# Moving operand, weight-sum and weight-split work inside a gated-MLP / channel-MLP kernel on one core

## The chip, the cores and the metric

The kernel runs on one core of one Trainium2 chip. A core has four compute engines that the profile names PE (matrix products), DVE, ACT and POOL (GpSimd), a queue SP that issues nearly all transfers of this kernel, and 16 DMA engines that carry them. The metric is the time of one execution on the device, in microseconds (us); lower is better.

## The reference, cut to what matters

```python
def reference(...):
    attn_out = favor attention of q, k, v            # 8 batches, 8 heads, 576 tokens
    x = attn_out as [8, 576, 512]
    # gated MLP
    h = relu(x @ w_in); u, v = halves of h
    v_n = normalised v over its features
    gated = u * (w_spatial @ v_n + b_spatial)
    x = gated @ w_out
    # token mixing of rank 32, then channel MLP
    u = x + (x^T @ U @ V)^T
    ch = relu(u @ w_ch1) @ w_ch2                      # 512 -> 2048 -> 512
    return u + ch
```

The inputs `w_ch1` and `w_ch2` come in a 64-bit form that the kernel must first turn into float32; it calls that fetching or repacking a weight.

## The kernel before, in words

The kernel runs in three parts, one behind the other: attention (to about 420 us), the gated MLP, batch by batch for 8 batches of some 63 us, and the channel MLP. The last batch of the gated MLP overlaps with the start of the channel MLP.

Every product is made in split precision. `split` makes a high part of an operand (a cast, on ACT at line 145 or on DVE at line 147) and a low part (source minus high part, line 148, on DVE in all places that matter here), and `products` multiplies three combinations of them.

The channel MLP uses seven block products where a 2 x 2 block product has eight (`PRODUCTS`). Left operands are sums of weight blocks, formed on POOL by `left_sums` (line 437, four operations a block) and then split into tiles `cw` (first matrix, also called w1) or written to memory as `w2d` and loaded again as `w` (second matrix). Right operands are sums of activation blocks: `right_parts` loads a batch as `u`, forms the differences `t` on POOL (`less`, line 1075) and splits the seven operands into tiles `us` (ACT, then DVE). What comes out of the inner products (`ph_x`, `ph_y`, `ph_z`) is added up on DVE as `c` (line 1138), goes through the ReLU on ACT as `h`, and becomes the right operand of the outer products, whose differences `t` (POOL) and splits `hc` (ACT, DVE) are made by `operands`. The outer products fill `pc`; DVE adds them to `r` (line 1300).

The hidden width of 2048 is taken in two halves of 1024. Each half and each of the 8 batches makes one outer pass, so there are 16, numbered from 0. A pass has 28 outer groups of six matmuls (`OUTER`: seven products, four tiles `t` each), and behind nearly every outer group one inner group of six matmuls of the pass to come. The program order in the channel MLP is written out by hand and kept (`put`): the order of the code is the order on each engine.

The weights are prepared in three places:

- In gated batches 1 to 6 `work()` is called eight times a batch (four times in the gate's first loop, twice in its second, twice around the mixing products), and each call does the next step of a job and, where that ends it, begins another. A job is the turning of a piece of `w_ch1` or `w_ch2` into float32 (`fetch_weight`: `raw_c` loaded, `low_c` and `bits_c` computed), or, for batches 1 to 4, `pair(m)`, which forms the first half's sums of w2 and stores them (`w2s` to `w2d`).
- The first half's w1 sums are made in the last gated batch, in the transition to the channel MLP: `fetch_pair(m)` loads the raw blocks `ca`, `combine(m)` forms the sums `cs` on POOL and splits both into `cw`, for m = 0 to 3.
- The second half's sums of both matrices are made by `second_group`, 41 steps of 8 weight blocks (one step of sums on POOL, four steps of splits `cd` on ACT and DVE whose results are stored). `channel` takes one step behind each of the seven outer products of a pass, from the middle of pass 0 on, until they are used up in pass 6.

`channel` first runs the inner products `7 * GROUP + LEAD - 7 * EARLY` steps ahead (six groups beyond the first batch's), then starts pass 0. In the last batch of the gated MLP `gated_out` makes each token tile's products `px`, copies them to `x` on ACT (line 940; the last product of a tile is line 770), splits `x` into `xh` and `xl` on DVE, and `low_rank` multiplies these into `pr`.

Of the kernel before, what the change touches and what calls it, by code (L numbers as in the profile page):

```python
# [9 lines left out]
F32 = mybir.dt.float32  # L10
# [8 lines left out]
P = 128  # L19
# [5 lines left out]
LEAD = 6  # L25

# [73 lines left out]
class Mixer:  # L100
# [3 lines left out]
    def __init__(self, tc, ctx, aps):  # L104
# [31 lines left out]
        self.w1x = dp.tile([P, GROUP, 2, 7, 2 * P], F32, name="w1x")  # L136
# [207 lines left out]
    def channel_jobs(self):  # L344
# [78 lines left out]
        jobs = jobs[3 * GROUP :]  # L423
        n = len(todo) - GROUP
        for i in range(n):
            todo[GROUP + i] = jobs[i::n]
# [438 lines left out]
    def gate(self, b, jobs):  # L865
# [27 lines left out]
        for f in range(self.KH):  # L893
# [20 lines left out]
            if f < self.KH - 2:  # L914
                self.work()
# [74 lines left out]
    def alloc_channel(self, es):  # L990
        tc = self.tc
        pool = lambda name: es.enter_context(
            tc.tile_pool(name=name, bufs=1, side="right")
        )
        cw, self.hu, hp, self.cst = [pool(n) for n in ("cw", "hu", "hp", "cst")]
        self.cw, self.hp = [cw] * 3, [hp]
        self.w1, self.h, self.us, self.raw = {}, {}, {}, {}

    def alloc_outer(self, es):
# [3 lines left out]
        self.cw.append(pool("cv"))  # L1003
        self.hp.append(pool("hq"))
        self.w2p, self.hc, self.ot = [pool(n) for n in ("w2p", "hc", "ot")]
        self.ps["c"] = pool("psc", space=PSUM, reuse_waits="tile")

    def fetch_raw(self, kind, m):

        a = self.cst.tile([P, 4, 2 * P], F32, tag="c32a", name=f"ca{kind}_{m}", bufs=1)  # L1010
# [12 lines left out]
    def fetch_pair(self, m):  # L1023
        self.raw[m] = self.fetch_raw(1, m)
# [5 lines left out]

    def combine(self, m):

        a = self.raw.pop(m)
        z = self.sums_of(a, m)
        w = self.first_left(m)
        flat = w.rearrange("p i x k c -> p i x (k c)")
        self.split(flat[:, 0, :3], flat[:, 1, :3], a[:, :3], elo="dve")
        self.split(flat[:, 0, 3:], flat[:, 1, 3:], z, elo="dve")

    def first_left(self, m):  # L1040
        t = m % GROUP
        w = self.cw[t].tile([P, 2, 7, 2, P], F32R, tag=f"w{t}", name=f"cw{m}", bufs=1)
        self.w1[m] = w
        return w

    def second_group(self):
# [5 lines left out]
        for n, (kind, m) in enumerate(blocks):  # L1052
# [3 lines left out]
            for x, k, src in ((0, 2, a[:, :2]), (2, 1, a[:, 2:3]), (3, 2, z[:, :2]), (5, 2, z[:, 2:])):  # L1056
                d = self.w2p.tile([P, 2, 2, 2 * P], F32R, tag="cd", name=f"cd{kind}_{m}_{x}", bufs=2)
                self.split(d[:, 0, :k], d[:, 1, :k], src, elo="dve")
                for i in range(2):
                    dst = (  # L1060
                        self.w1x[:, t, i, x : x + k, :] if kind == 1
# [16 lines left out]
    def right_parts(self, n, u):  # L1078
# [452 lines left out]
```

## Time and profile before

| | before |
|---|---|
| median of 3 runs | 1668.12 us (1666.5 to 1670.28) |
| the profiled execution's own time | 1674.35 us |
| its span in the trace | 1672.6 us |
| PE busy | 1589.4 us, 95% of the span |
| DVE busy | 1146.1 us, 69% |
| ACT busy | 877.5 us, 52% |
| POOL busy | 792.8 us, 47% |
| mean granted clock of PE over the span | 0.981 |

The span is what the profile shows from the first to the last instruction. The profiled execution took 1.75 us more than its span and 6.2 us more than the median of the timed runs. A busy PE is not always PE at full speed: where the granted clock is below 1.00, matmuls run longer, so both PE's idle time and its clock have to be read. A mean clock below 1.00 is a mixture of two levels, 2.4 and 1.2 GHz.

### The profile page before, as it was taken

Reading aid. Unit: us, or ns where it says so; the run is one execution under the profiler, and the core shown is the slowest. Engines: PE = TensorE matmul, PEld = TensorE weight load, DVE = VectorE, ACT = ScalarE, POOL = GpSimd, SP = SyncE. Lnnn points to the kernel's source line nnn. Section 1 sums busy time; section 2 is a strip of 40 time slices with the busy share of each in tenths; the row PEclk is TensorE's granted clock in tenths of the full one; section 3 lists DMA queues with packets and bytes.
Section 4 is the critical chain, followed back from the end, with each engine's and each line's share of the span. In section 5 each row is a group of like instructions: output and inputs, shape, how many; then the busy total and the mean of one; then the engine's idle time right before and its main releaser. Section 6 shows DMA issues by size and latency. Waiting matters only on the chain.

```text
span 1672.6 us, 30522 instructions
## 1 busy us (share of the span) xinstructions
PE 1589.4 (95%) x11592; PEld 1484.4 (89%) x11592; DVE 1146.1 (69%) x1642; ACT 877.5 (52%) x1668; POOL 792.8 (47%) x610
## 2 busy tenths in 40 slices
PE   7999999999999999999997989999989999999998
PEld 7998988988889789788786889999989999999998
DVE  5888757855567767757637567777766776666665
ACT  4888767873344344344334455555544455444453
POOL 2678766774334334334234436654543444443442
PEclk9999999999999999999997999999999999999999
DMA  4677766642143343343213669889989867777776
GB/s 131 178 208 206 205 185 185 195 139 86 56 154 106 106 154 103 109 123 91 84 58 116 198 215 302 294 289 310 305 285 374 263 219 230 233 250 241 244 239 231
DMA packets 169302, 322.04 MB, mean 193 GB/s; under 512 B 25474, under 2 KB 96290, under 8 KB 166596
## 3 DMA queue, kind: packets, MB, share of 16 engines
q1 hardware_dynamic: 169012, 320.03, 60.4%
q8 instruction: 91, 1.49, 0.4%
q14 instruction: 55, 0.45, 0.1%
q10 hardware_dynamic: 144, 0.07, 0.0%
HBM read 244.24 MB, written 66.21 MB: 186 GB/s over the span
## 4 chain that ended last, share of the span: by engine, by line
PE 61%; DVE 12%; DMA 10%; ACT 7%; issue 5%; POOL 4%; SPq 1%; DVEq 0%; POOLq 0%; ACTq 0%
PE pc L758 16%; PE ph_x L758 9%; PE pn L595 4%; PE ph_z L758 4%; PE pv L758 4%; PE pkv L567 4%; PE pu L758 3%; DMA raw_c<-in_w_ch 3%; POOL t L1075 2%; PE ph_y L758 2%; PE px L758 2%; DVE us L148 2%; PE pk L494 2%; DMA w<-w2d 2%; PE pt L526 1%
## 5 line engine op out<-in xcount | busy, mean ns | idle before, releaser
L758 PE MATMUL pc<-hc,w 128*128 128x288 f32 x2688 | 427.1, 298 | 9.7 <-DVE hc L148 3.7
L758 PEld LDWEIGHTS pc<-hc,w 128*128 128x128 f32 x2688 | 383.8, 190 | 12.4 <-ACT hc L145 4.8
L758 PE MATMUL ph_x<-us,cw 128*128 128x288 f32 x1536 | 252.0, 301 | 12.6 <-ACT u L1133 10.6
L548 POOL TENSOR_TENSOR qp<-e,qp 128x576 fp32r<-128x576 f32 x128 | 183.5, 1455 | 120.6 <-ACT e L545 94.8
L758 PEld LDWEIGHTS ph_x<-us,cw 128*128 128x128 f32 x1536 | 222.2, 192 | 16.9 <-ACT u L1133 13.6
L1075 POOL TENSOR_TENSOR t<-h,h 128x576 f32<-128x576 f32 x64 | 95.7, 1496 | 254.0 <-DVE hc L148 223.9
L595 PE MATMUL pn<-qp,kv 128*65 128x288 f32 x768 | 207.7, 331 | 7.7 <-DVE nd L604 4.0
L148 DVE TENSOR_TENSOR hc<-t,hc 128x576 fp32r<-128x576 f32 x128 | 127.0, 994 | 76.9 <-ACT hc L145 76.2
L567 PE MATMUL pkv<-v,kp 128*128 128x65 f32 x1024 | 155.2, 255 | 0.0
L567 PEld LDWEIGHTS pkv<-v,kp 128*128 128x128 f32 x1024 | 153.9, 194 | 0.0
L1146 ACT ACTIVATE h<-c 128x288 f32<-128x288 f32 x192 | 85.6, 446 | 127.9 <-DVE c L1138 127.8
L1133 ACT COPY u<-ph_x 128x288 f32<-128x288 f32 x128 | 51.0, 398 | 171.5 <-PE ph_x L758 171.1
L758 PE MATMUL ph_z<-us,cw 128*128 128x288 f32 x768 | 126.7, 301 | 11.9 <-DVE c L1138 11.9
L758 PEld LDWEIGHTS ph_z<-us,cw 128*128 128x128 f32 x768 | 110.4, 191 | 15.4 <-DVE c L1138 15.1
L148 DVE TENSOR_TENSOR hc<-h,hc 128x576 fp32r<-128x576 f32 x96 | 116.6, 1230 | 3.4 <-ACT hc L145 3.1
L1075 POOL TENSOR_TENSOR t<-h,t 128x576 f32<-128x576 f32 x64 | 112.0, 1751 | 8.3 <-DVE hc L148 5.8
L1075 POOL TENSOR_TENSOR t<-u,t 128x576 f32<-128x576 f32 x32 | 56.7, 1773 | 124.5 <-DVE us L148 123.2
L758 PE MATMUL pz<-wt,vn 128*128 128x288 f32 x768 | 112.7, 296 | 0.2
L595 PEld LDWEIGHTS pn<-qp,kv 128*65 128x65 f32 x768 | 99.6, 140 | 13.5 <-ACT nd L606 5.6
L758 PE MATMUL pu<-xs,wi 128*128 128x288 f32 x768 | 104.8, 298 | 3.6 <-DVE v L822 3.6
L758 PEld LDWEIGHTS pu<-xs,wi 128*128 128x128 f32 x768 | 104.1, 190 | 4.6 <-DVE v L822 3.9
L1300 DVE TENSOR_TENSOR r<-pc,r 128x576 f32<-128x576 f32 x112 | 84.5, 755 | 33.2 <-PE pc L758 31.9
(169 smaller groups left out, 3166.4 us busy)
## 6 DMA issues: line engine op xcount, KB each, us to landing
w<-w2d SPq DMA_DIRECT2D x224, 512.0 KB, 4.6
u<-ud SPq DMA_DIRECT2D x16, 1152.0 KB, 5.8
raw_c<-in_w_ch SPq DMA_DIRECT2D x32, 512.0 KB, 4.1
v<-in_v SPq DMA_DIRECT2D x32, 325.0 KB, 4.1
k<-in_kT SPq DMA_DIRECT2D x32, 320.0 KB, 3.4
q<-in_qT SPq DMA_DIRECT2D x32, 320.0 KB, 4.1
x<-nd SPq DMA_DIRECT2D x64, 144.0 KB, 3.4
rec<-rd SPq DMA_DIRECT2D x64, 144.0 KB, 3.2
```

What stands on the lines that cost most here:

```text
L148: return self.put((nc.gpsimd if elo == "pool" else nc.vector).tensor_tensor(out=lo, in0=src, in1=hi, op=ALU.subtract))
L494: self.pin(nc.tensor.matmul(pa[:, j * NF + t, :], x[d, t * P : (t + 1) * P], ws[d, :], start=True, stop=True,))
L526: self.pin(nc.tensor.transpose(pt[:, at, :], s[:, u, :], self.ident))
L548: self.pin(nc.gpsimd.tensor_tensor(out=lo[:, c], in0=e[:, c], in1=hi[:, c], op=ALU.subtract))
L567: self.pin(nc.tensor.matmul(pkv[:, i, j, :], kp[:, j * NF + t, :], vb[:, u * D1 : (u + 1) * D1], start=False, stop=(j == 1 and t == NF - 1),))
L595: self.pin(nc.tensor.matmul(pn, kv[k][:, i, g // 2, :], qp[q][:, i, g * HS : (g + 1) * HS], start=(m == 0), stop=(m == len(terms) - 1),))
L758: self.put(self.nc.tensor.matmul(out, x, y, start=(start and i == 0), stop=(stop and i == len(terms) - 1), skip_group_check=chained,))
L1075: self.put(self.nc.gpsimd.tensor_tensor(out=out, in0=p, in1=q, op=ALU.subtract))
L1133: self.put(nc.scalar.copy(out, src))
L1146: self.put(nc.scalar.activation(self.h[n, t // 2, x][:, t % 2], src, AF.Relu))
L1300: self.put(nc.vector.tensor_tensor(out=r, in0=pc, in1=r, op=ALU.add))
```

## The change

Five things are changed.

1. The first half's w1 sums move from the transition into gated batch 6. A new job `left(m)` loads the raw blocks, forms the sums, splits them in two parts (tiles `w1s`) and stores them in `w1x[0]`; the last batch then only loads the four finished tiles with `load_left`. `fetch_pair`, `combine` and `first_left` are gone. Batches 1 to 4 now repack four pieces and do a `pair` (before three and a `pair`), batch 5 repacks the last eight, and batch 6 does the four `left` jobs (before, batches 5 and 6 repacked six pieces each in turn). `work()` is called once more in a batch, in the gate's second loop.
2. `right_parts` forms the next batch's operands in another order (product 2 before product 1; `t3` before the split of product 1 and `t6` behind it), and begins at inner product (2, 2) instead of (3, 0), so its steps are spread over 16 inner products instead of 11.
3. The 41 weight steps of the second half are taken at outer groups 0, 2, 4, ..., 12 of the 28 of a pass, from pass 1 on, instead of at every fourth group of the whole pass from the middle of pass 0 on. They still end in pass 6.
4. Pass 0 begins four inner groups sooner (`FIRST = 2` instead of 6 ahead); the four are made up behind its groups 3, 7, 11 and 15. In the first products (2, 0) moves behind (1, 5) and (1, 6).
5. Pools: `cw`'s four tags stand in one pool, `h` in pools by pair and by parity, and `cst` is taken with the outer pools. The numbers of buffers are in effect the same.

The core of the diff:

```diff
@@ channel_jobs
-        todo = [[] for _ in range(self.B - 2)]
-        for m in range(GROUP):
-            todo[m] = jobs[3 * m : 3 * m + 3] + [pair(m)]
...
+        def left(m):
+            def load():
+                w = self.mq.tile([P, 4, self.DM // 2], F32, tag="w2", name=f"w1_{m}", bufs=1)
+                self.raw_blocks(w, 1, m)
+                return lambda: sums(w)
+            def sums(w):
+                z = self.mq.tile([P, 4, self.DM // 2], F32, tag="z2", name=f"z1_{m}", bufs=1)
+                self.left_sums([w[:, x] for x in range(4)], z)
+                return part(w, z, 0)
+            def part(w, z, k):
+                n, src = (4, z) if k else (3, w[:, :3])
+                d = self.mq.tile([P, 2, 4, self.DM // 2], F32R, tag="w2s", name=f"w1s_{m}_{k}", bufs=1)
+                self.split(d[:, 0, :n], d[:, 1, :n], src, elo="dve")
+                for i in range(2):
+                    nc.sync.dma_start(
+                        self.w1x[0][:, m, i, 3 * k : 3 * k + n], d[:, i, :n].bitcast(F32)
+                    )
+                return (lambda: part(w, z, 1)) if k == 0 else None
+            return load
+        todo = [jobs[4 * m : 4 * m + 4] + [pair(m)] for m in range(GROUP)]
+        todo += [jobs[4 * GROUP :], [left(m) for m in range(GROUP)]]
@@ gate
-            if f < self.KH - 2:
+            if f < self.KH - 1:
                 self.work()
@@ new
+    def load_left(self, m):
+        g, t = divmod(m, GROUP)
+        w = self.cw.tile([P, 2, 7, 2, P], F32R, tag=f"w{t}", name=f"cw{m}", bufs=1)
+        self.nc.sync.dma_start(
+            w.bitcast(F32).rearrange("p i x k c -> p i x (k c)"), self.w1x[g][:, t]
+        )
+        self.w1[m] = w
@@ right_parts
+        part(2, t1)
+        yield
+        t3 = self.less(new(3), b22, b12)
+        yield
         part(1, t2)
         yield
-        part(2, t1)
         t6 = self.less(t2, b21, t2)
-        yield
-        t3 = self.less(new(3), b22, b12)
@@ inner
-        spread = {(3, 0), (2, 5), (3, 2), (3, 3), (3, 4), (4, 0), (3, 5), (3, 6), (4, 1)}
+        begin = {(2, 3): 1, (2, 5): 1, (2, 6): 1, (3, 6): 2, (4, 0): 2, (4, 2): 1, (4, 3): 1, (4, 4): 1}
+        spread = {
+            x: 1 for x in (
+                (2, 2), (2, 4), (2, 5), (3, 2), (3, 3), (3, 4), (4, 0), (3, 5), (4, 1), (4, 3),
+            )
+        }
@@ channel
-        for _ in range(7 * GROUP + LEAD - 7 * EARLY):
+        for _ in range(7 * GROUP + FIRST - 7 * EARLY):
             next(inner, None)
...
-                    for _ in range((0, 1, 0, 3)[t] if x == 3 else 1):
+                    pulls = (0, 1, 0, 3)[t] if x == 3 else 1
+                    at = GROUP * OUTER.index(x) + t
+                    if n == 0 and at in (3, 7, 11, 15):
+                        pulls += (LEAD - FIRST) // 4
+                    for _ in range(pulls):
                         next(inner, None)
-                if n or OUTER.index(x) > 2:
-                    next(later, None)
+                    if n and at in range(0, 14, 2):
+                        next(later, None)
@@ last gated batch
-            mx.fetch_pair(0)
-            right_parts = mx.right_parts(0, mx.load_chunk(0))
+            u = mx.load_chunk(0)
+            for m in range(GROUP):
+                mx.load_left(m)
+            right_parts = mx.right_parts(0, u)
```

Below, the orders of instructions on an engine show what the change moves. A name such as `hc_5_0` is a tile of outer product 5; the long number behind a name is a counter.

DVE in pass 2, before, behind the outer products whose sums are `r_11`; `us_4` are splits of the next batch's operands, `cd` a weight step's split, and `c_3` the sum that frees the bank for which a later inner product `ph_z` waits:

```order
L1300 TENSOR_TENSOR r_11_11550<-pc_0_11483,r_11_11550 128x576
L1300 TENSOR_TENSOR r_11_11550<-pc_2_11728,r_11_11550 128x576
L148 TENSOR_TENSOR us_4_11869<-u_4_11541,us_4_11869 128x576
L148 TENSOR_TENSOR us_4_11879<-t_4_11767,us_4_11879 128x576
L148 TENSOR_TENSOR us_4_11890<-t_4_11765,us_4_11890 128x576
L148 TENSOR_TENSOR cd_6_5_11894<-cs_6_11561,cd_6_5_11894 128x512
L148 TENSOR_TENSOR hc_5_0_11899<-h_2_0_10907,hc_5_0_11899 128x576
L1138 TENSOR_TENSOR c_3_11919<-ph_3_z,u_3_11888 128x288
L148 TENSOR_TENSOR us_4_11937<-t_4_11921,us_4_11937 128x576
L148 TENSOR_TENSOR hc_5_1_11940<-h_2_2_11187,hc_5_1_11940 128x576
L1138 TENSOR_TENSOR c_3_11957<-ph_3_z,u_3_11866 128x288
```

The same place after:

```order
L1320 TENSOR_TENSOR r_11_11569<-pc_0_11487,r_11_11569 128x576
L1320 TENSOR_TENSOR r_11_11569<-pc_2_11751,r_11_11569 128x576
L149 TENSOR_TENSOR us_4_11896<-t_4_11728,us_4_11896 128x576
L149 TENSOR_TENSOR us_4_11916<-t_4_11730,us_4_11916 128x576
L149 TENSOR_TENSOR hc_5_0_11919<-h_2_0_10911,hc_5_0_11919 128x576
L1153 TENSOR_TENSOR c_3_11939<-ph_3_z,u_3_11914 128x288
L149 TENSOR_TENSOR us_4_11956<-t_4_11906,us_4_11956 128x576
L149 TENSOR_TENSOR hc_5_1_11959<-h_2_2_11219,hc_5_1_11959 128x576
L1153 TENSOR_TENSOR c_3_11976<-ph_3_z,u_3_11893 128x288
```

Ahead of `hc_5_0` and `c_3` stand now two splits `us_4` where three splits and a `cd` stood; the first of the three (from `u_4`) and the `cd` are taken earlier in the pass. In the passes without weight steps the same place reads the same without the `cd` lines.

DVE at the beginning of the last gated batch's mixing, before; `cw` and `ca`, `cs` belong to `combine`, `xh` and `xl` to the token tiles that `low_rank` waits for, `us_0` to the first batch's operands:

```order
L148 TENSOR_TENSOR cw_9707<-ca_0_9656,cw_9707 128x768
L148 TENSOR_TENSOR cw_9707<-cs_9702,cw_9707 128x1024
L147 CAST xh_0_9694<-x_0_9693 128x512
L147 CAST xh_1_9722<-x_1_9721 128x512
L148 TENSOR_TENSOR xl_0_9695<-x_0_9693,xh_0_9694 128x512
L148 TENSOR_TENSOR xl_1_9723<-x_1_9721,xh_1_9722 128x512
L148 TENSOR_TENSOR us_0_9730<-u_0_9661,us_0_9730 128x576
L147 CAST xh_2_9734<-x_2_9733 128x512
L148 TENSOR_TENSOR us_0_9742<-u_0_9661,us_0_9742 128x576
L148 TENSOR_TENSOR xl_2_9735<-x_2_9733,xh_2_9734 128x512
```

The same place after:

```order
L148 CAST xh_0_9775<-x_0_9774 128x512
L149 TENSOR_TENSOR xl_0_9776<-x_0_9774,xh_0_9775 128x512
L148 CAST xh_1_9788<-x_1_9787 128x512
L148 CAST xh_2_9800<-x_2_9799 128x512
L149 TENSOR_TENSOR xl_1_9789<-x_1_9787,xh_1_9788 128x512
L149 TENSOR_TENSOR xl_2_9801<-x_2_9799,xh_2_9800 128x512
L149 TENSOR_TENSOR us_0_9796<-u_0_9734,us_0_9796 128x576
L149 TENSOR_TENSOR us_0_9808<-u_0_9734,us_0_9808 128x576
L148 CAST xh_3_9812<-x_3_9811 128x512
L149 TENSOR_TENSOR us_0_9830<-t_0_9783,us_0_9830 128x576
```

The splits of `cw` are gone and the token tiles' splits stand first.

ACT in gated batch 6, around the copies of `px` to `x`, before; `low_c` belongs to the repacking of a weight and waits for the load of `raw_c`:

```order
L61 ACTIVATE low_c_14_8955<-raw_c_14_8917 128x512
L780 COPY gt_9039<-g_8870 128x4x64 x2
L79 ACTIVATE low_c_14_8955<-raw_c_14_8917 128x512
L61 ACTIVATE low_c_15_9239<-raw_c_15_8965 128x512
L940 COPY x_0_9089<-px_0_9059 128x512
L940 COPY x_1_9098<-px_1_9069 128x512
L940 COPY x_2_9107<-px_2_9079 128x512
L79 ACTIVATE low_c_15_9239<-raw_c_15_8965 128x512
L940 COPY x_3_9116<-px_3_9118 128x512
```

The same place after:

```order
L800 COPY gt_9114<-g_8939 128x4x64
L146 CAST w1s_0_9027<-w_2_8981 128x768
L800 COPY gt_9114<-g_8939 128x4x64
L146 CAST w1s_1_9068<-z_2_9022 128x1024
L960 COPY x_0_9164<-px_0_9134 128x512
L960 COPY x_1_9173<-px_1_9144 128x512
L960 COPY x_2_9182<-px_2_9154 128x512
L960 COPY x_3_9191<-px_3_9193 128x512
```

No `low_c` stands ahead of the copies any more; the casts there belong to the second and third `left` job, whose sources were loaded and summed earlier in the batch.

## Rows read from the trace of the kernel before

**Rows 1.** The page, busy time of each engine.
```profile
PE 1589.4 (95%) x11592; PEld 1484.4 (89%) x11592; DVE 1146.1 (69%) x1642; ACT 877.5 (52%) x1668; POOL 792.8 (47%) x610
```

**Rows 2.** Windows by stage: length, busy time (instructions) of five engines, clock, DMA share, GB/s.
```profile
863.68:936.22 72.54, 57.86 (x299) 48.75 (x297) 46.44 (x59) 35.29 (x74) 34.73 (x28) 0.86 0.44 144
...
974.75:1027.83 53.08, 46.82 (x337) 45.92 (x337) 36.44 (x46) 25.38 (x56) 27.41 (x22) 0.97 0.81 264
1027.83:1173.05 145.22, 138.75 (x1008) 138.06 (x1008) 109.44 (x137) 75.96 (x165) 78.40 (x53) 0.96 0.89 296
...
1218.47:1272.44 53.97, 47.98 (x336) 46.88 (x336) 32.09 (x44) 24.64 (x54) 22.69 (x17) 0.94 0.89 324
1272.44:1593.75 321.31, 315.55 (x2352) 312.04 (x2352) 220.49 (x280) 159.48 (x344) 135.48 (x85) 1.00 0.76 247
```

**Rows 3.** Timeline of PE, three places in the passes; in brackets idle before, releaser.
```profile
945.66 0.96 PE L758 MATMUL ph_z<-us,cw 128*128 128x288 f32 x6
...
953.60 0.95 PE L758 MATMUL ph_y<-us,cw 128*128 128x288 f32 x6
...
1076.24 1.24 PE L758 MATMUL ph_z<-us,cw 128*128 128x288 f32 x6 [2.16 <-DVE c L1138]
...
1318.35 1.06 PE L758 MATMUL ph_z<-us,cw 128*128 128x288 f32 x6 [0.35 <-DVE c L1138]
...
1325.45 1.06 PE L758 MATMUL ph_x<-us,cw 128*128 128x288 f32 x6 [0.47 <-ACT u L1133]
```

**Rows 4.** Timeline of DVE behind the outer sums of a pass with weight steps.
```profile
1072.02 1.93 DVE L148 TENSOR_TENSOR cd<-cs,cd 128x512 fp32r<-128x512 f32 x1
1073.87 1.95 DVE L148 TENSOR_TENSOR hc<-h,hc 128x576 fp32r<-128x576 f32 x1
```

**Rows 5.** Timeline of a pass without weight steps, POOL beside DVE.
```profile
1405.62 0.76 DVE L148 TENSOR_TENSOR us<-u,us 128x576 fp32r<-128x576 f32 x1 [0.58 <-ACT us L145]
...
1407.12 2.00 POOL L1075 TENSOR_TENSOR t<-u,t 128x576 f32<-128x576 f32 x1 [8.65 <-DVE us L148]
...
1407.74 1.99 DVE L148 TENSOR_TENSOR hc<-h,hc 128x576 fp32r<-128x576 f32 x1
```

**Rows 6.** Transition: timelines of ACT, POOL and PE; the DVE groups of tile cw.
```profile
873.32 1.05 ACT L145 CAST cw<-cs 128x1024 fp32r<-128x1024 f32 x1 [3.57 <-POOL cs L437]
874.27 1.55 ACT L940 COPY x<-px 128x512 f32<-128x512 f32 x3
...
874.52 2.40 POOL L1075 TENSOR_TENSOR t<-u 128x576 f32<-128x576 f32 x1 [1.23 <-DMA u<-ud]
...
879.94 0.50 PE L956 MATMUL pr<-xl,ub 128*128 128x512 f32 x1 [2.18 <-DVE xl L148]
...
914.15 1.60 PE L758 MATMUL ph_x<-us,cw 128*128 128x288 f32 x10 [1.69 <-DVE cw L148]
...
L148 DVE TENSOR_TENSOR cw<-ca,cw x4: 948/1454/2185, 869.8 to 911.9; 128x768 fp32r<-128x768 f32 x4
...
L148 DVE TENSOR_TENSOR cw<-cs,cw x4: 1209/1226/2429, 874.4 to 914.0; 128x1024 fp32r<-128x1024 f32 x4
```

**Rows 7.** Gated batch 6: timelines of ACT and PE, one window.
```profile
811.05 0.66 ACT L61 ACTIVATE low_c<-raw_c 128x512 int32<-128x512 uint32 x1 [4.32 <-DMA raw_c<-in_w_ch]
...
812.24 3.78 PE L770 MATMUL px<-wo,gt 128*128 128x512 f32 x8 [3.71 <-ACT x L940]
...
800.00:820.00 20.00, 16.29 (x61) 12.44 (x60) 12.21 (x24) 6.68 (x13) 0.99 (x1) 0.83 0.32 93
```

**Rows 8.** DMA issues: count, KB each, median us to landing; window of highest load.
```profile
w<-w2d SPq DMA_DIRECT2D x224, 512.0 KB, 4.6
...
cw<-w1x SPq DMA_DIRECT2D x4, 1792.0 KB, 10.9
w1x<-cd SPq DMA_DIRECT2D x24, 256.0 KB, 4.3
...
1240.00:1260.00 20.00, 19.38 (x147) 19.17 (x146) 9.92 (x16) 10.59 (x23) 9.57 (x6) 1.00 1.03 391
```

More of the change, by code (lines that the diff above doesn't have):

```diff
@@ L135, in __init__ @@
         ]
-        self.w1x = dp.tile([P, GROUP, 2, 7, 2 * P], F32, name="w1x")
+        self.w1x = [dp.tile([P, GROUP, 2, 7, 2 * P], F32, name=f"w1x{g}") for g in range(2)]
         self.pinning = False
@@ L994, in alloc_channel @@
         )
-        cw, self.hu, hp, self.cst = [pool(n) for n in ("cw", "hu", "hp", "cst")]
-        self.cw, self.hp = [cw] * 3, [hp]
-        self.w1, self.h, self.us, self.raw = {}, {}, {}, {}
+        self.cw, self.hu, hp = [pool(n) for n in ("cw", "hu", "hp")]
+        self.hp = {(0, 0): hp}
+        self.w1, self.h, self.us = {}, {}, {}
     def alloc_outer(self, es):
@@ L1021, in fetch_raw @@
         return a
-    def fetch_pair(self, m):
-        self.raw[m] = self.fetch_raw(1, m)
+    def fetch_raw(self, kind, m):
+        a = self.cst.tile([P, 4, 2 * P], F32, tag="c32a", name=f"ca{kind}_{m}", bufs=1)
+        return self.raw_blocks(a, kind, m)
     def sums_of(self, a, name):
@@ L1029, in sums_of @@
         return z
[L1031 to L1044, printed above, removed]
     def second_group(self):
@@ L1142, in keep @@
             if t % 2 == 0:
[L1143 to L1144 removed]
+                self.h[n, t // 2, x] = self.hp[t // 2, n % 2].tile(
+                    [P, 2, HS], F32, tag=f"h{x}{n % 2}", name=f"h{x}_{n}_{t}", bufs=1
                 )
@@ L1207, in inner @@
                 u = self.load_chunk(n + 1)
-            if (t, i) == (3, 0) and u is not None:
+            if (t, i) == (2, 2) and u is not None:
                 right, u = self.right_parts(n + 1, u), None
-            if (t, i) in spread or t == 0 and (4, i) in spread and n:
+            at, steps = (k, i), begin
+            if k > GROUP + 1 or k == GROUP + 1 and i < 5:
+                at, steps = (t, i), spread
+                if t == 0 and (GROUP, i) in spread:
+                    at = (GROUP, i)
+            for _ in range(steps.get(at, 0)):
                 next(right, None)
             if i == 6 and (n + 1) % B == 0 and g + 1 < groups:
-                self.nc.sync.dma_start(
-                    self.first_left((g + 1) * GROUP + t).bitcast(F32).rearrange(
-                        "p i x k c -> p i x (k c)"
-                    ),
-                    self.w1x[:, t],
-                )
+                self.load_left((g + 1) * GROUP + t)
             yield
@@ L1427, in favor_gmlp_mixer_kernel @@
             ts.append(mx.gated_out(b, t, begun[t] if t < 3 else None))
-            if last and t == 0:
-                mx.combine(0)
-                mx.fetch_pair(1)
             parts(1)
@@ L1433, in favor_gmlp_mixer_kernel @@
         mx.low_rank(pr, ts, range(3))
-        if last:
-            mx.combine(1)
-            mx.fetch_pair(2)
         ahead(2)
@@ L1443, in favor_gmlp_mixer_kernel @@
         ahead(1)
-        if last:
-            mx.combine(2)
-            mx.fetch_pair(3)
         mx.work()
```

21 lines of the change are left out of this document (7 added, 14 removed).

## The prediction

> **What bounds the kernel now.** I read the page first. PE is busy for 95% of the span and no other engine for more than 69% [rows 1], so only two things can shorten the time: idle time of PE, and time in which PE runs below full clock. I then cut the span by stage and looked in each for PE's busy time beside the length, and for the clock [rows 2], and read PE's timeline for what ends its waits [rows 3].
>
> A plain pass of the channel MLP, with no weight steps, is the yardstick. Seven of them take 321.31 us, 45.90 each [rows 2]. Ten groups of six matmuls lie between the first two rows of PE's timeline, 953.60 - 945.66 = 7.94 us, so 0.794 a group [rows 3], and 56 groups would take 44.5. A plain pass thus loses 1.4 us, in two waits of 0.35 and 0.47 and what follows them [rows 3].
>
> Against that yardstick three stages lose time:
>
> - The transition, 863.68 to 936.22: 72.54 us with PE busy for 57.86 at a clock of 0.86 [rows 2]. That is 14.7 us of idleness, and (1 - 0.86) x 72.54 = 10.2 us lost to the clock, 24.9 in all.
> - Passes 1 to 6, which carry the weight steps: 974.75 to 1272.44 [rows 2], 297.7 us, where six plain passes take 275.4. 22.3 us are lost against a plain pass.
> - Gated batch 6: one wait of 3.71 us and a clock of 0.83 over 20 us, 3.4 us, together 7.1 [rows 7].
>
> A mean clock of 0.86 is a mixture of 2.4 GHz and the lower level of 1.2 GHz, so a share of 0.28 of that stretch ran at half speed. Half speed is visible behind waits: the first ph_z after the 2.16 us wait takes 1.24 us where the same instruction takes 1.06 behind a wait of 0.35 [rows 3], and the transition's low clock goes with its many short waits. So a wait that goes can give back more than its length.
>
> **The change part by part.** All terms are set against the profiled execution, 1674.35 us; it ran 6.2 us above the median of the timed runs, which I subtract at the end.
>
> *Gated MLP.* In batch 6 ACT holds a repacking step that waits 4.32 us for raw_c, and the copies of px stand behind it; PE's last products of the tile wait 3.71 us for them [rows 7]. After the change the casts ahead of these copies belong to jobs whose data was loaded earlier, so the wait and the low clock behind it go: -7.1. On the other side, batches 1 to 4 repack one piece more, in a ninth call that stands where PE is near the same copies. The trace shows no such batch. From below it costs nothing (the steps are on ACT, DVE and POOL, which are idle for a good part of a batch), from above 3.71 each, the row of batch 6. Most calls stand beside 60 us of matmuls, so I take 0.8 each, 3.1 in all. Net -4, between -7 and +8.
>
> *Transition.* Gone are eight casts of cw on ACT, eight splits of cw on DVE (four of 1.45 and four of 1.23 by their medians, some 11 us [rows 6]) and sixteen sums on POOL. What they hold up: the copies of px to x begin at 874.27 on ACT because a cw cast ahead of them waited 3.57 us for POOL's sum, then took 1.05 [rows 6]. Behind that, pr waits 2.18 us for DVE's xl; a later inner product waits 1.69 for a cw split directly [rows 6]. In the new order xh and xl stand first on DVE. What comes in their place: four loads of 1792 KB, which took 10.9 us each later in the kernel [rows 8]; the next limit is then u, whose arrival lets POOL begin at 874.52 [rows 6], and which has not moved. So the start cannot come forward without limit. Of the 24.9 us lost I expect the x copies' delay (some 4), the cw waits (some 3), and, with fewer waits, half of the clock's 10.2 and a little of the other idle time: -14. Bounds: -5 if only the waits on cw and half the copies' delay go and the clock falls all the same, -22 if nearly the whole loss goes.
>
> *Weight steps and operands in passes 1 to 6.* Three of these passes have the wait of 2.16 us for c of which one stands in [rows 3]. The reason stands in DVE's queue: a split cd of 1.93 us and then an hc of 1.95 stand ahead of that c [rows 4]. After the change the cd and the first of three us are no longer there, which shortens the queue by more than the wait; what is late next is what is late in a plain pass, 0.35 us. Passes 1 and 6, with the remainder of the loss, have POOL's weight sums ahead of the differences t; these too move to the first part of the pass. So up to 22.3 us can be had. What it costs: the seven steps a pass now fall into 13 of 28 outer groups, 20.7 us. A full step stores two pieces of 256 KB [rows 8]; a whole block stores what a later cw load fetches, 1792 KB [rows 8], and reads four raw blocks, 512 KB by their shapes. Seven of the 41 steps of eight blocks are 7/41 x 8 x 2304 = 3147 KB a pass: 67 GB/s over the 48.4 us of a pass before (145.22 / 3 [rows 2]) and 156 over 20.7 after. The DMA engines carry 296 GB/s in these passes [rows 2], so they would come to some 385 in the first half; the highest that a stretch shows is 391, at a share of 1.03 [rows 8]. The loads of w land in 4.6 us at the median [rows 8] and are issued four tiles ahead, 16 groups or 12.7 us. That is cover, but near the limit it shrinks, and I take 1.5 us a pass for it: 22.3 - 6 x 1.5 = 13.3, rounded to -13, between -3 and -22.
>
> *Operands in plain passes.* One us less in front of c gives back at most the two waits, 0.82 x 7 = 6 us; but t6 now comes later on POOL, and the second wait, which ACT ends, may hang on it. What speaks against a gain is how DVE and POOL meet: a split alone takes 0.76 us, and one that starts while POOL works takes 1.99, ending after POOL's operation of 2.00 [rows 5]. The Trainium skill, in "SBUF — State Buffer", section "Who interferes with whom", has the rule for it: DVE's operation with two SBUF inputs and a GpSimd one that reads SBUF take turns on a shared port. By the trace it holds here. The number of operations stays the same, only the partners change, so I take 0, between -6 and +8.6 (1.23 us, 1.99 - 0.76, in each of seven passes).
>
> *The earlier start of pass 0 and the pools.* No instruction is added. Pass 0's four missing inner groups are made up inside it, where DVE has the time that the removed cw split left. Taken at 0; the bound is a wait like 2.16 on either side.
>
> Sum: -4 - 14 - 13 + 0 + 0 = -31. 1674.35 - 31 = 1643.4, and minus 6.2 for the median 1637.
>
> **Rivals.**
>
> *The transfers become the bound in the first halves of passes 1 to 6, moderately.* For it: 385 beside 391 GB/s. Against it: at 391 PE still was busy for 19.38 of 20 us [rows 8]. Then only 3 of the 13 are gained, 1647.
>
> *The collisions between DVE and POOL move ahead of awaited sums.* Seven plain passes and six others each lose 1.23 us: +16, 1653. The rule of the Trainium skill named above would make it so wherever a difference on POOL starts just before an hc that c waits behind; no row shows whether it will.
>
> *Slower.* If the DMA engines can't hold more than 296 GB/s beside this work, then in every pass 20.7 us of the first part stretch by 385/296, by 6.2 us, and PE's clock falls behind the waits as in batch 6, by 3.4 [rows 7]. That is 6 x 9.6 = 58 on top of a plain pass, against the 22 that go: the passes lose 36 instead of gaining 13, and the sum is -4 - 14 + 36 = +18, 1686. It decides as soon as w's landing passes 12.7 us. Against it stands the window of 391 GB/s.
>
> *The move out of the transition brings nothing.* If u and the cw loads, not the splits, set the first inner products, only -5 remains of the 14: 1646.
>
> *All works and the clock stays up.* 22 + 22 + 7 = 51: 1617.
>
> **How the numbers follow.** Forecast (1626 to 1644) 0.5; transfers moderately the bound or the transition without effect 0.18; collisions 0.1; the clock stays up 0.09; two of the gains missing and a loss in batches 1 to 4, so no change, 0.05; slower 0.08, by the transfers or by losses in the gated batches that I could not bound better. The predicted time is the likeliest's, 1637. The range leaves out the slowest and the very fastest: 1619 to 1660. A change is told from none here at about 0.2%, 3.3 us: faster 0.5 + 0.18 + 0.1 + 0.09 = 0.87, same 0.05, slower 0.08.
>
> **What would show it.** Right: batch 6 without the 3.7 us wait and at full clock; no cw split in the transition, pr's waits under 1 us, and a clock above 0.9 there; passes 1 to 6 at 46 to 48 us each, with no wait of 2 us for c. Wrong: PE waiting for w in the first half of a pass; x copies late in batches 1 to 4; pr still waiting for xl at 2 us; plain passes longer than 45.9.

## The result and the profile after

The changed kernel takes 1655.15 us (median of 4 runs, 1652.56 to 1655.4); before takes 1669.2 us beside it (4 runs). The ratio is 0.9914, with an interval of [0.9896, 0.9932]: faster by 14 us, where 31 were forecast. A second comparison, on another chip, gave 0.9948 [0.9931, 0.9965], 1653.69 us beside 1661.76. The kernel before scatters from run to run (25 runs there lie between 1655.05 and 1669.11), and the last section shows one reason.

The profiled execution of after took 1655.13 us with a span of 1653.3. The page's row of busy time:

```profile
PE 1574.3 (95%) x11592; PEld 1467.8 (89%) x11592; DVE 1177.9 (71%) x1642; ACT 879.0 (53%) x1668; POOL 793.9 (48%) x610
```

Set beside [rows 1], PE is busy for 15 us less, with the same 11592 matmuls: the work is the same and ran at a higher clock (0.992 on average, where it was 0.981). The other 4 us of the span's 19.3 are idle time.

Where the time went and came from is seen by cutting both timelines at the same places: the first px product of the first gated batch, that of the last one, the wait of PE for ACT's u that ends pass 0, and the same wait six passes later. All lengths are in us, each the difference of two starts in PE's timeline.

| kernel | attention | seven gated batches | transition and pass 0 | six passes with weight steps | rest |
|---|---|---|---|---|---|
| before | 422.8 | 440.9 | 121.6 | 294.3 | 393.1 |
| after | 423.8 | 452.8 | 100.3 | 285.5 | 390.9 |
| difference | +1.0 | **+11.9** | **-21.3** | **-8.9** | -2.1 |

The prediction's windows [rows 2] cut its passes elsewhere, at a ph_z that PE starts 7.1 us ahead of that wait (969.82 and 1255.27 in after). At the end of pass 0 before, two waits of 1.74 and 1.86 us lie between the two cuts:

```profile
974.75 1.06 PE L758 MATMUL ph_z<-us,cw 128*128 128x288 f32 x6 [0.35 <-DVE c L1138]
...
982.44 0.93 PE L758 MATMUL pc<-hc,w 128*128 128x288 f32 x5 [1.74 <-DVE hc L148]
985.23 1.81 PE L758 MATMUL ph_x<-us,cw 128*128 128x288 f32 x6 [1.86 <-ACT u L1133]
```

By the prediction's cut the transition and pass 0 went from 111.1 to 93.2 us, -17.9, and the six passes from 297.7 to 285.5, -12.2.

Four windows of after, in the columns of [rows 2]: gated batch 2, the transition up to the first pc, the six passes, and seven plain passes.

```profile
549.94:614.94 65.00, 61.28 (x357) 53.07 (x358) 48.49 (x86) 28.55 (x59) 25.18 (x24) 1.00 0.42 130
876.64:925.41 48.77, 44.41 (x276) 39.29 (x274) 26.96 (x45) 25.77 (x59) 10.45 (x7) 1.00 0.72 280
976.92:1262.38 285.46, 273.24 (x2017) 268.14 (x2017) 229.62 (x273) 151.03 (x327) 152.46 (x105) 1.00 0.91 313
1262.38:1581.66 319.28, 315.76 (x2353) 312.44 (x2353) 230.73 (x281) 159.49 (x344) 134.15 (x85) 1.00 0.76 246
```

The transition's clock went from 0.86 to 1.00. The plain passes take 319.28 / 7 = 45.61 us, where they took 45.90. The six passes came out at 47.6 on average, 2.0 above a plain one. Gated batch 2, 65.0 us long, has lost 3.7 us that no row of the clock explains. PE's timeline of that place:

```profile
549.94 11.50 PE L778 MATMUL px<-wo,g 128*128 128x512 f32 x48 [1.20 <-DVE u L928]
563.66 2.11 PE L790 MATMUL px<-wo,gt 128*128 128x512 f32 x8 [2.21 <-ACT x L960]
...
567.37 0.50 PE L976 MATMUL pr<-xl,ub 128*128 128x512 f32 x1 [0.23 <-DVE xl L149]
```

PE waits 2.21 us for ACT's copy of px to x, then 0.23 more for xl; batches 1, 3 and 4 have the same wait at 2.01, 2.08 and 1.97. ACT's timeline beside it:

```profile
562.07 1.04 ACT L146 CAST w2s<-z 128x1024 fp32r<-128x1024 f32 x1 [4.40 <-DMA w2d<-w2s]
563.02 2.04 ACT L960 COPY x<-px 128x512 f32<-128x512 f32 x4
```

The four copies stand behind the second cast of the job `pair`, and that cast waits 4.40 us for a store: it writes into the one tile w2s, out of which the first half's results are still being stored.

In the passes with weight steps the 2.16 us wait of [rows 3] is gone, but a new one stands earlier in the pass. POOL, DVE and PE in pass 3:

```profile
1095.14 1.96 POOL L1089 TENSOR_TENSOR t<-u 128x576 f32<-128x576 f32 x1
...
1095.72 2.00 DVE L149 TENSOR_TENSOR us<-u,us 128x576 fp32r<-128x576 f32 x1
...
1097.63 1.90 DVE L149 TENSOR_TENSOR cd<-cs,cd 128x512 fp32r<-128x512 f32 x1
1099.45 0.45 DVE L1153 TENSOR_TENSOR c<-ph_z,u 128x288 f32<-128x288 f32 x1
...
1099.95 1.05 PE L778 MATMUL ph_z<-us,cw 128*128 128x288 f32 x6 [1.72 <-DVE c L1153]
```

PE waits 1.72 us for a c that ended at 1099.90; ahead of it on DVE stand a us of 2.00 (more than two and a half times the 0.76 of [rows 5], beside POOL's t) and the cd of the step at group 12, 1.90. And the beginnings of pass 0 and of two plain passes on PE:

```profile
925.41 0.40 PE L778 MATMUL pc<-hc,w 128*128 128x288 f32 x1 [1.16 <-ACT hc L146]
928.56 1.57 PE L778 MATMUL pc<-hc,w 128*128 128x288 f32 x5 [2.76 <-DVE hc L149]
...
1262.38 1.05 PE L778 MATMUL ph_x<-us,cw 128*128 128x288 f32 x6 [0.48 <-ACT u L1148]
...
1307.96 1.06 PE L778 MATMUL ph_x<-us,cw 128*128 128x288 f32 x6 [0.48 <-ACT u L1148]
```

Pass 0 begins with waits of 1.16 and 2.76 us. In the plain passes one wait of 0.48 is left; that of 0.35 is gone.

### The profile page after: what moved, and what is told of

Its sections match the earlier page's. It is cut to its first block, busy times and chain, and to the rows that moved or that the text cites. A ratio compares the mean times of both kernels' runs of the same rounds, so it can differ in the third digit from the quotient of the medians.

```text
span 1653.3 us, 30606 instructions
## 1 busy us (share of the span) xinstructions
PE 1574.3 (95%) x11592; PEld 1467.8 (89%) x11592; DVE 1177.9 (71%) x1642; ACT 879.0 (53%) x1668; POOL 793.9 (48%) x610
## 4 chain that ended last, share of the span: by engine, by line
PE 53%; DVE 17%; DMA 14%; ACT 8%; issue 4%; POOL 2%; SPq 1%; DVEq 0%; ACTq 0%; POOLq 0%
PE pc L778 12%; PE ph_x L778 7%; PE pn L615 5%; PE pv L778 4%; PE pu L778 4%; PE pkv L587 4%; PE ph_z L778 4%; DVE hc L149 3%; DVE us L149 3%; DMA w<-w2d 2%; DMA w2d<-cd 2%; PE ph_y L778 2%; PE pk L514 2%; PE pt L546 2%; DMA raw_c<-in_w_ch 1%
## 5 line engine op out<-in xcount | busy, mean ns | idle before, releaser
L778 PE MATMUL pc<-hc,w 128*128 128x288 f32 x2688 | 422.4, 296 | 6.7 <-ACT hc L146 2.8
L778 PEld LDWEIGHTS pc<-hc,w 128*128 128x128 f32 x2688 | 379.2, 188 | 8.8 <-ACT hc L146 4.5
L778 PE MATMUL ph_x<-us,cw 128*128 128x288 f32 x1536 | 247.1, 296 | 9.8 <-ACT u L1148 7.0
L778 PEld LDWEIGHTS ph_x<-us,cw 128*128 128x128 f32 x1536 | 217.6, 188 | 14.4 <-ACT u L1148 10.9
L1089 POOL TENSOR_TENSOR t<-u 128x576 f32<-128x576 f32 x32 | 49.8, 1558 | 136.0 <-DVE us L149 116.6
L149 DVE TENSOR_TENSOR us<-t,us 128x576 fp32r<-128x576 f32 x64 | 85.0, 1331 | 36.1 <-ACT us L146 35.3
```

The costliest lines, as they stand in the source:

```text
L149: return self.put((nc.gpsimd if elo == "pool" else nc.vector).tensor_tensor(out=lo, in0=src, in1=hi, op=ALU.subtract))
L778: self.put(self.nc.tensor.matmul(out, x, y, start=(start and i == 0), stop=(stop and i == len(terms) - 1), skip_group_check=chained,))
L1089: self.put(self.nc.gpsimd.tensor_tensor(out=out, in0=p, in1=q, op=ALU.subtract))
```

## The experiments

The times by stage of all runs, cut as in the table above, with the ratio to before that was measured beside each. The stages are those of one profiled execution; it took 7.7 us more than the median for "late call, change 2 undone", 6.9 for "after, once more", 4.2 for "change 2 alone", and is within 4 us of it for the others. So two or three us between stages of two rows can be the executions' own: the two traces of after differ by 2.4 us in the rest.

| kernel | gated | transition, pass 0 | six passes | rest | median | ratio to before |
|---|---|---|---|---|---|---|
| change 1 alone | 454.5 | 106.0 | 293.3 | 393.2 | 1666.24 | 1.0014 [0.9996, 1.0031] |
| changes 2 to 4 alone | 437.3 | 114.9 | 284.7 | 391.6 | 1650.06 | 0.9914 [0.9894, 0.9935] |
| change 2 alone | 438.6 | 118.2 | 296.4 | 391.6 | 1662.06 | 0.9998 [0.9977, 1.0019] |
| change 3 alone | 439.1 | 115.1 | 278.0 | 393.8 | 1648.59 | 0.9913 [0.988, 0.9945] |
| after, once more | 452.9 | 100.7 | 284.8 | 393.3 | 1653.69 | 0.9948 [0.9931, 0.9965] |
| after, change 4 undone | 454.6 | 105.0 | 286.4 | 391.1 | 1658.32 | 0.9969 [0.9949, 0.9989] |
| after, six steps a pass | 453.5 | 100.3 | 283.0 | 394.5 | 1653.05 | 0.9933 [0.9913, 0.9953] |
| after, ninth call late | 435.0 | 101.6 | 285.3 | 390.8 | 1635.36 | 0.9824 [0.9802, 0.9846] |
| after, three pieces | 442.8 | 111.6 | 286.1 | 393.5 | 1654.45 | 0.995 [0.9935, 0.9965] |
| late call, change 2 undone | 435.1 | 105.6 | 282.6 | 395.6 | 1638.48 | 0.9861 [0.9832, 0.9889] |
| late call, hybrid | 435.6 | 105.6 | 278.0 | 389.8 | 1629.62 | 0.9818 [0.9788, 0.9849] |
| late call, hybrid behind batch 2 | 434.9 | 101.9 | 279.3 | 390.1 | 1628.28 | 0.9787 [0.9766, 0.9809] |

**Change 1 alone.** The operands, the weight steps and the start of pass 0 are put back as in before.

```diff
-FIRST = 2
+FIRST = LEAD
... (right_parts, the first products and inner: as in before)
-                    if n and at in range(0, 14, 2):
-                        next(later, None)
+                if n or OUTER.index(x) > 2:
+                    next(later, None)
```

> Change 1 alone (first half's w1 sums in gated batch 6, with the pools of change 5); operands, weight steps and the start of pass 0 are as before. Theory: the trace of after shows the gated batches 11.9 us longer and the transition some 20 us shorter, and both belong to this change, so about -9 against before, 1660, with waits of 2 us for ACT's x copies in batches 1 to 4. Rival: most of the transition's gain comes from the earlier pass 0 and the operands' new order; then this kernel is no faster than before, 1669 to 1675.

Measured: no difference from before. PE's timeline, in batch 2 and where pass 0 begins:

```profile
561.68 3.69 PE L790 MATMUL px<-wo,gt 128*128 128x512 f32 x8 [2.06 <-ACT x L960]
...
932.47 0.61 PE L778 MATMUL pc<-hc,w 128*128 128x288 f32 x1 [1.11 <-ACT hc L146]
```

The theory was half right: its stages are there (gated +13.5, transition and pass 0 -15.6), but nothing is left of them in sum. The rival was right about the total, for another reason than it gave, since the transition did get shorter by 15.6 without changes 2 to 4.

**Changes 2 to 4 alone**, on before.

> Changes 2 to 4 without change 1. Theory: passes 0 to 6 gain 6 to 9 us and plain passes 2, the gated batches and the transition stay as before, so about -8 to -10, 1660. Rival: the transition's gain belongs here, then -20 or more, under 1650.

The ratio is that of after itself. The gain of the whole change is thus the gain of these parts; the six passes are 9.6 us shorter, and the transition and pass 0 6.7. With -13.9 us by the medians it lies between the theory and the rival. The gated batches take 3.6 us less than in the trace of before, though their program is the same.

**The ninth call behind the mixing.** Only the place of a call changes:

```diff
@@ gate
-            if f < self.KH - 1:
+            if f < self.KH - 2:
                 self.work()
@@ behind the second half of the mixing products
+        mx.work()
```

> After, with the ninth work call of a batch moved from the gate's second loop to behind the mixing products. Theory: in batches 1 to 4 the second w2s cast then stands behind the copies of px to x on ACT, so the waits of 2.0 to 2.2 us of PE for x go and with them the small waits for xl; four batches give back 2 to 3 us each, in all -8 to -12, 1645. Rival: the batches got longer because of the fourth piece's work on DVE and ACT as such, wherever its call stands; then 1655 as after, or less than 2 us off it.

The ratio fell from 0.9914 to 0.9824, more than expected, and the gated batches from 452.8 to 435.0. ACT in batch 2:

```profile
552.65 1.55 ACT L960 COPY x<-px 128x512 f32<-128x512 f32 x3
557.97 1.05 ACT L146 CAST w2s<-z 128x1024 fp32r<-128x1024 f32 x1 [3.76 <-DMA w2d<-w2s]
558.92 0.58 ACT L960 COPY x<-px 128x512 f32<-128x512 f32 x1
```

PE at the same place, and the batch's window:

```profile
554.64 2.00 PE L790 MATMUL px<-wo,gt 128*128 128x512 f32 x8
```

```profile
543.67:605.16 61.49, 60.30 (x357) 53.28 (x358) 48.58 (x86) 28.64 (x59) 24.84 (x24) 1.00 0.44 137
```

The cast still waits for its store, 3.76 us, but three copies of x are ahead of it, and PE's last products of the tiles start without a wait. The batch takes 61.49 us instead of 65.00. The work is the same; so the place of the call, and not the fourth piece's work, cost the 3.5 us. The call moves steps on ACT and DVE together; that the cast on ACT is the one that counts is read from PE's wait, which ACT's copy ends. From batch 4's px to batch 5's 7.0 us came back, with the clock at 1.00 instead of 0.97; from batch 5's to batch 6's only 0.7, with the clock still at 0.97.

**Six steps a pass**: `range(0, 12, 2)` instead of `range(0, 14, 2)`.

> After, with weight steps at outer groups 0 to 10 only, six a pass, so that they end in pass 7 instead of 6. Theory: the cd split of the step at group 12 stands ahead of the sum c for which the inner product waits (1.72 us in pass 3), so passes 1 to 6 lose about 1 us less each and pass 7 has a little more: -4, 1651. Rival: the load on DMA and POOL in the first half sets the loss of these passes, and fewer steps a pass change less than 1.5 us.

The ratio lies between those of after's two measurements, so nothing was gained where -4 was expected. PE's timeline, in passes 4 and 5, then 6 and 7:

```profile
1157.88 1.06 PE L778 MATMUL ph_x<-us,cw 128*128 128x288 f32 x6 [0.49 <-ACT u L1148]
...
1203.64 1.05 PE L778 MATMUL ph_x<-us,cw 128*128 128x288 f32 x6 [0.48 <-ACT u L1148]
...
1240.14 1.82 PE L778 MATMUL pc<-hc,w 128*128 128x288 f32 x12 [1.33 <-DMA w<-w2d]
...
1284.84 1.06 PE L778 MATMUL ph_z<-us,cw 128*128 128x288 f32 x6 [1.01 <-DVE c L1153]
```

The waits for c are gone from passes 4 and 5, which take 45.6 and 45.8 us, as the theory says. Pass 6 then waits 1.33 us for w and takes 51.7 (49.5 in after), and pass 7, which now has steps, has a wait of 1.01 for c. The six passes gain 2.4 us, and pass 7 takes 47.9 us where it took 45.6, so it gives 2.3 back.

**Change 2 alone**, on before.

> Before with change 2 alone (order and spread of the next operands). Theory: in plain passes the first wait (0.35 us) goes, in passes with weight steps the wait of 2.16 us falls to about 1.4, since one split us of 0.76 us leaves the queue ahead of that c; together -5 to -7 against before. Rival: the plain passes' gain comes from the pools or the earlier pass 0; then the waits of 0.35 us stay and there is nothing to be measured.

```profile
1069.85 1.05 PE L758 MATMUL ph_z<-us,cw 128*128 128x288 f32 x6 [1.68 <-DVE c L1139]
...
1082.34 1.06 PE L758 MATMUL ph_z<-us,cw 128*128 128x288 f32 x6 [1.10 <-DVE c L1139]
```

The wait of 2.16 is 1.68, and one of 1.10 stands new behind it. Plain passes fell to 45.5 us (the 0.35 went, without the pools and the early start), and still the median is that of before, where -5 to -7 was expected: the six passes with weight steps are together 2.1 us longer. That this is the operands' order is not shown, for in this execution PE waits 8.0 us for w in three waits, where in before it waits 2.2 in two; why the loads came later is open.

**Change 3 alone**, on before.

> Before with change 3 alone (weight steps at groups 0 to 12, from pass 1 on). Theory: the waits of 2.16 us fall to 0.35 and new ones of 1 to 1.7 us come behind the step at group 12, so passes 1 to 6 gain some 5 us, plain passes nothing: -5. Rival: without the operands' new order the new waits are larger and eat the gain: within 2 us of before.

Against the expectation there are no new waits behind the step at group 12. PE at the end of a pass with steps, and the window of the six passes:

```profile
1060.17 1.06 PE L758 MATMUL ph_z<-us,cw 128*128 128x288 f32 x6 [0.35 <-DVE c L1138]
...
1067.29 1.05 PE L758 MATMUL ph_x<-us,cw 128*128 128x288 f32 x6 [0.50 <-ACT u L1133]
```

```profile
975.47:1253.44 277.97, 271.35 (x2016) 267.67 (x2016) 221.55 (x273) 151.28 (x327) 153.66 (x105) 1.00 0.91 322
```

These are the waits of a plain pass, and 277.97 us is 2.6 above six of them. The DMA engines carry 322 GB/s here, more than the 313 of after, and PE waits for no w. This part alone has the ratio of the whole change, where -5 us was expected. The transition and pass 0 are 6.5 us shorter too: 3.4 of it are the two waits of 1.74 and 1.86 us at the end of pass 0, which carries no steps any more, and 3.0 lie ahead of pass 0's first pc, where the program is that of before.

**Change 4 undone**, in after: `FIRST = LEAD`, and (2, 0) ahead of (1, 5).

> The changed kernel with change 4 undone: pass 0 begins after 34 inner products and (2, 0) stands ahead of (1, 5). Theory: the four inner groups only move (3.2 us from pass 0 into the transition) and the waits at the start of pass 0 (1.16 and 2.76 us) come with the early start, so the time stays that of after within 2 us. Rival: the early start is what shortens the transition by the 6 us beyond the moved work that changes 2 to 4 alone show; then 4 to 6 us slower than after.

The rival was right: 1658.32 beside 1653.69 on the same chip, and 4.3 us in the stage. PE before pass 0:

```profile
926.94 1.17 PE L778 MATMUL ph_x<-us,cw 128*128 128x288 f32 x5 [1.35 <-DVE us L149]
...
930.42 3.01 PE L778 MATMUL ph_x<-us,cw 128*128 128x288 f32 x11 [0.32 <-DVE us L149]
934.55 0.61 PE L778 MATMUL pc<-hc,w 128*128 128x288 f32 x1 [1.11 <-ACT hc L146]
936.09 1.57 PE L778 MATMUL pc<-hc,w 128*128 128x288 f32 x5 [0.93 <-DVE hc L149]
```

With four more inner groups ahead of pass 0, PE waits for operands us (1.35, and the 3.01 us for eleven matmuls are at a granted clock of 0.50, 1.2 GHz) before it waits for hc. In after no such wait for us stands ahead of pass 0.

**Three pieces in batches 1 to 4**, without the ninth call there; seven in batch 5, five in batch 7.

```diff
@@ channel_jobs
-        todo = [jobs[4 * m : 4 * m + 4] + [pair(m)] for m in range(GROUP)]
-        todo += [jobs[4 * GROUP :], [left(m) for m in range(GROUP)]]
+        todo = [jobs[3 * m : 3 * m + 3] + [pair(m)] for m in range(GROUP)]
+        todo += [jobs[12:19], [left(m) for m in range(GROUP)], jobs[19:]]
... (the ninth call only from batch 6 on; batch 7 takes jobs too)
```

> The changed kernel with three pieces and a pair in gated batches 1 to 4 (no ninth call there), seven pieces in batch 5, the left jobs in batch 6 and five pieces in batch 7's gate. Theory: it is the fourth piece that pushes the pair's last cast behind a store and ahead of ACT's copies of px; batches 1 to 4 come back to what they took before, two of them with waits of some 0.6 us for x, and the time falls by 6 to 9 us against the changed kernel, about 1647. Rival: the casts stand ahead of the copies in any case and wait for the store, so the waits of 2 us stay in all four: 1653.

The gated batches are 10 us shorter, with waits for x of 0.6 to 0.7 in two of them, as the theory says; but the time is that of after, since the transition lost 11. PE in batch 3, and in the transition; then SP's queue:

```profile
615.47 2.12 PE L790 MATMUL px<-wo,gt 128*128 128x512 f32 x8 [0.67 <-ACT x L960]
...
885.69 0.80 PE L974 MATMUL pr<-xh,ua 128*128 128x512 f32 x1 [10.12 <-DVE xh L149]
```

```profile
863.87 7.03 SPq L359 DMA_DIRECT2D w2r<-w_c  x2
873.02 0.32 SPq L1085 DMA_DIRECT2D u<-ud  x1
```

The load of u stands on SP behind a store of a repacked piece that held the queue for 7.03 us. It was issued at 873.02, 13.3 us after the batch's first px; in after it is 1.7. DVE's us splits then wait for u, and the last xh of the token tiles stands behind them: 10.12 us.

**Change 2 undone, with the late call**, and then a **hybrid** in which the batches formed beside weight steps have the old order and spread, the others the new; last, the same with the **first two batches** in the new order too. From the edit of the last, where `old` chooses the order of before:

```diff
@@ right_parts
+        if 2 <= n <= 8:
+            part(1, t2)
...
@@ inner
+            old = GROUP + 2 <= k <= 8 * GROUP + 1
+            if (t, i) == ((3, 0) if old else (2, 2)) and u is not None:
```

> The kernel with the ninth work call behind the mixing, with change 2 undone: operands in the order and spread of before; changes 1, 3, 4 and 5 stay. Theory: passes 1 to 6 become as short as with the weight steps alone (278 us instead of 285 to 286), since the waits of up to 1.75 us for c came from the operands' earlier splits meeting the weight steps on DVE; plain passes get 0.3 us longer each. Together -5 against that kernel, about 1630. Rival: the transition needs the new order, and loses as much as the passes gain: 1635 as with it.

> As the run before, but the new operands' order and spread are kept for the batches formed in the passes without weight steps. Theory: passes 1 to 6 at 278 us and plain passes at 45.6 us, so 2 us below the run before, about 1628. Rival: the plain passes' waits depend on something else that change 2 set up, and it equals the run before.

> As the hybrid, but the first two batches' operands in the new order and steps too, so that the old order stands only for the six batches that are formed beside weight steps. Theory: the start of pass 0 gets back the waits of 1.2 and 2.75 us instead of 3.6 and 3.9, transition and pass 0 take 101 to 102 us instead of 105, passes 1 to 6 stay at 278: 1625 to 1627. Rival: the third batch's operands, formed in the old order behind the second's in the new one, come late, and pass 1 or 2 loses what pass 0 gains: 1629.

The first is not told apart from the late call alone, where 5 us less were expected: the intervals of the ratios overlap. Its passes 1 to 4 take 45.9 to 46.0 us each, as expected; in pass 6 of this execution PE waits 2.75 us for w, so that the six passes together are only 2.7 us shorter. The transition and pass 0 lose 4, as the rival says, and the rest is 4.8 longer, where plain passes account for 2.5. The hybrid has the six passes at 278.0, as expected, and the plain passes at 45.6. Its start of pass 0:

```profile
906.21 0.61 PE L778 MATMUL pc<-hc,w 128*128 128x288 f32 x1 [3.63 <-ACT hc L146]
910.76 1.57 PE L778 MATMUL pc<-hc,w 128*128 128x288 f32 x5 [3.94 <-DVE hc L149]
```

With the first two batches in the new order these waits are 1.17 and 2.75 again, and the window of the six passes is:

```profile
956.06:1235.36 279.30, 271.83 (x2017) 267.75 (x2017) 219.55 (x273) 151.18 (x327) 153.72 (x105) 1.00 0.91 321
```

1.3 us longer than in the hybrid, in pass 6 with two waits for w (0.23 and 1.94). This version, 1628.28 us, is not told apart from the hybrid, but it beats both kernels, after by more than 1%.

## Why the prediction missed the size

**The step that failed is the gated MLP's term.** The text took 0.8 us for each of batches 1 to 4, since "most calls stand beside 60 us of matmuls", in all -4 with bounds of -7 and +8 (four times 0.8 is 3.2, not 3.1, which changes nothing). Measured: +11.9. From the first px of one batch to that of the next the three kernels take, in us:

| kernel | 0 to 1 | 1 to 2 | 2 to 3 | 3 to 4 | 4 to 5 | 5 to 6 | 6 to 7 |
|---|---|---|---|---|---|---|---|
| before | 60.2 | 64.8 | 60.7 | 65.1 | 60.4 | 63.0 | 66.7 |
| after | 61.3 | 64.8 | 65.0 | 64.9 | 66.9 | 67.6 | 62.4 |
| after, ninth call late | 61.3 | 61.5 | 61.5 | 61.5 | 59.9 | 66.9 | 62.4 |

Batches 1 to 4, with a `pair` each, took 251.0 us together before, 261.5 after and 244.3 with the late call: 2.6 us more each than before, not 0.8. Batch 5 took 4.6 more, and batch 6, whose wait went as foretold, 4.3 less where 7.1 were put down. In batches 4 and 5 of after the clock was 0.97, some 1.7 us each. Batches 1 and 3 are no longer than before, because they lost time there already: PE waits 1.12 us for u among the px and 0.65 for x. The kernel before has the same cast in the same place. Its ACT and PE in batch 1, then in batch 2:

```profile
494.61 1.05 ACT L145 CAST w2s<-z 128x1024 fp32r<-128x1024 f32 x1 [3.63 <-DMA w2d<-w2s]
...
496.19 2.12 PE L770 MATMUL px<-wo,gt 128*128 128x512 f32 x8 [0.65 <-ACT x L940]
...
556.80 1.05 ACT L145 CAST w2s<-z 128x1024 fp32r<-128x1024 f32 x1 [3.10 <-DMA w2d<-w2s]
...
558.83 2.01 PE L770 MATMUL px<-wo,gt 128*128 128x512 f32 x8
```

So "the trace shows no such batch" was not the whole of it: in the trace of before this cast already waits 3.63 and 3.10 us for its store with the copies of x behind it, and PE waits 0.65 us or not at all. In after the cast starts 12.1 us behind batch 2's first px, where it started 9.0 behind, and PE waits some 2 us in all four batches. I priced a call by the length of the work beside it; what counts is which instruction stands ahead of the copies of x on ACT, what that one waits for, and how late it comes. The late call shows it: the same work with three copies ahead of the cast takes 6.7 us less than before in batches 1 to 4. It leaves the 5 to 6 column at 66.9, so the loss there has another cause, for which the prediction had no term. In the late call's trace PE waits 3.88 us there for a t of DVE; nothing tests it, and it stays open.

**Transition and pass 0: -14 and 0 were forecast; by the prediction's cut -17.9 came.** The part from the sums is -15.6 (change 1 alone, the same by either cut), and -12.6 against the trace of change 3 alone, which has the program of before up to pass 0; so the term was right. The early start, taken at 0, is worth 4.3 (change 4 undone). The two do not add up exactly.

**The six passes: -13 was forecast, by the prediction's cut -12.2 came, and the price I put on it was the wrong one.** Of the 22.3 us that could be had, change 3 alone took 19.7 (297.7 to 278.0 by this cut). I took 1.5 us a pass for w's loads. Change 3 alone moves as many bytes in the same places and has no waits for w; in after PE waits for w once, 0.78 us in pass 6. What costs 1.2 us a pass is change 2: with the operands begun earlier, a us and a cd meet ahead of a c, and DVE's operations stretch beside POOL's. From the late call to its hybrid the six passes fall from 285.3 to 278.0, and PE's waits for c in them from 7.8 us to 1.8. So the term came near its size by luck: a cost of one kind was taken off, one of another kind was paid. That was a rival's mechanism ("collisions"), with its 1.23 us a pass close to the mark, but in the passes with steps and not in the plain ones; that its 1653 lies near the measured time is chance too, for it has no loss in the gated batches. The rule of the Trainium skill in "SBUF — State Buffer", section "Who interferes with whom", says that a DVE instruction with two SBUF inputs contends with a GpSimd one that reads SBUF. The us of 2.00 beside a t of 1.96 in after agrees with it.

**Plain passes: 0 was forecast, -0.3 each came,** the first wait of [rows 3], within the bounds.

**The base.** I took the sum from one execution and subtracted its 6.2 us above the median at the end, as if both kernels had it. By the two traces the gain is 19.2 us, by the medians 14. The profiled execution of before had a clock of 0.981, below the 25 runs on the second chip (0.983 to 0.990); some 5 us of what the terms could win back were that execution's own. They lie ahead of pass 0: change 3 alone, whose program is that of before up to there, reaches pass 0's first pc at 929.84 us instead of 936.22, 1.5 us less in the attention, 1.8 in the gated batches and 3.0 in the transition. Set against that trace, the gated batches lost 13.7 us, and the transition and pass 0 won 14.9 by the prediction's cut.

So of the -31, the transition and the passes together gave -30.1 where -27 were forecast; the gated batches took 11.9 back, and 5 were never there for the medians.

## What to carry to other kernels

When background work is moved into a stage that has room by its busy shares, price it by the first instruction behind it that the busy engine waits for: look up in the order what stands ahead of that instruction, and for each of these what it waits for, a store out of its only buffer included. Look first for the same instruction in the trace of the kernel before: here it stood ahead of the copies already, with little room left. Changes to the same queue don't add: the operands' new order won 0.3 us in passes without weight steps, cost 1.2 in passes with them, and the best version uses each where it fits. And test a bundle by its parts, since one part alone here had the whole gain, and another hid a gain of 15.6 us behind a loss of 13.5.

## What the runs showed of the hardware that was not expected

The attention part is the same in all kernels, yet the first gated px started between 416.97 and 427.09 us. The same stretches of time in the two traces at these ends, after once more and the one with three pieces:

```profile
240.00:320.00 80.00, 76.57 (x721) 70.62 (x723) 59.11 (x70) 59.69 (x83) 52.07 (x39) 0.96 0.62 181
320.00:400.00 80.00, 74.67 (x599) 66.59 (x595) 48.59 (x76) 51.94 (x87) 53.07 (x44) 0.96 0.47 138
400.00:417.00 17.00, 14.51 (x99) 14.51 (x100) 11.84 (x28) 6.57 (x21) 6.02 (x6) 0.90 0.08 28
```

```profile
240.00:320.00 80.00, 79.27 (x775) 72.39 (x773) 62.21 (x74) 65.41 (x93) 53.20 (x40) 1.00 0.67 193
320.00:400.00 80.00, 71.17 (x556) 63.76 (x555) 48.84 (x80) 46.89 (x81) 51.66 (x42) 0.98 0.42 122
400.00:417.00 17.00, 17.00 (x130) 16.96 (x129) 11.48 (x27) 11.98 (x32) 10.85 (x9) 1.00 0.45 143
```

The clock is 0.96, 0.96 and 0.90 in the one, 1.00, 0.98 and 1.00 in the other, with PE busy for 71 to 79 of 80 us in the four long windows. By these clocks 8.1 us are lost in the one (0.04 of 80, 0.04 of 80 and 0.10 of 17 us) and 1.6 in the other, an estimate of 6.5 of the 10 us between them. Why the same program gets a lower clock in one execution is not shown, so small changes are better read from the stages than from the total.
